# Pooled attention into a snake MLP on one core: k loaded by halves of the heads and ahead of the moves, q paired to suit, and the rest of the first batch moved

## Chip, core, metric

The kernel runs on one core of a Trainium2 chip. The metric is device microseconds of one execution. Engine names are those of the profile: PE is TensorE's matmuls, PEld its weight loads, DVE VectorE, ACT ScalarE, POOL GpSimd, and SPq the queue from which SyncE issues transfers.

## The reference

Attention pools k and v by means of 8 tokens (576 tokens to 72), and its output, reshaped to 4608 x 512, feeds an MLP with the activation h + sin(alpha h)^2 / alpha.

```python
def _attn_ref(q, k, v):                    # 8 batches, 8 heads, 576 tokens, 64 per head
    k_p = k.reshape(B, H, 72, 8, D).mean(axis=3)
    v_p = v.reshape(B, H, 72, 8, D).mean(axis=3)
    attn = softmax(q @ k_p^T / sqrt(D))    # abridged
    return attn @ v_p

def _moe_ref(x, w_in, w_out, alpha):       # 4608 x 512, 512 x 2048, 2048 x 512
    h = x @ w_in
    g = h + sin(alpha * h) ** 2 / (alpha + 1e-09)
    return g @ w_out
```

## The kernel before

The first MLP product runs in nine units, each of 28 slots of eight matmuls (1.73 us a slot at full clock). Attention of batch u + 1 is threaded through unit u: a table says at which slot each of its steps is put into the instruction streams. Every queue executes in the order of that table. "Cut" marks what is left out.

```python
def load_k(self, b, e):                    # half the heads of a batch: 4 heads x 24 rows of 6 KB
    t = self.kvp.tile([P, 2048], F32, name="kvin")[:NP * m, 0:3 * POOL * D]
    self.nc.sync.dma_start(out=t, in_=self.k[b].rearrange("(hp e) (p x) d -> e hp p (x d)", e=2, x=3 * POOL)[e])
    # cut: self.kp[b]
    self.pool_rows(t.rearrange("p (j x) -> p j x", j=3), self.kp[b][:, :, e, :])   # three additions on GpSimd

def move(part):                            # the softmax, transposed in blocks by VectorE, into place: 16 small transfers a batch
    for a in (2 * part, 2 * part + 1):
        for s in range(2):
            for c in range(2):
                nc.sync.dma_start(out=flat(self.aM[r:r + 32, a]), in_=flat(tr[32 * a:32 * a + 32, c, s]))

# the table for unit u, batch b = u + 1 (cut)
at((1, 3, 4, 5, 6)[i], A.score, i)         # scores and the subtraction of the maximum
at((8, 9, 10, 10, 10)[i], A.exp, i)
at((9, 10, 10, 10, 11)[i], A.norm, i)
at((11, 12, 12, 13, 13)[i], A.turn, i)     # VectorE's block transposes
at(13, A.move, 0)
at(13, A.move, 1)
at((0, 1)[i], self.load_v, b, i)
at((14, 15)[i], self.load_k, b + 1, i)     # behind the moves in the SP queue
at(25, lambda: A.values((0, 2, 1, 3), A.free_banks()))
at(26, self.att[b + 1].k_t)                # TensorE transposes the pooled k of the next batch
turn = 21                                  # q of batch u + 2: transposes on VectorE at slots 21, 22, transfers at 23, 24

# unit 0 also (cut)
at(2, A0.score, 4); at(2, A0.exp, 4); at(2, A0.norm_rest)    # the last 64 tokens of batch 0, its "rest"
at(3, self.root)                           # 1/sqrt(alpha): VectorE, a square root on ScalarE, VectorE
at((4, 10, 14)[J - 1], self.combine_w_in, J, 0)
at((6, 12, 15)[J - 1], self.combine_w_in, J, 1)              # three additions on VectorE, both inputs in SBUF
at((4, 5)[i], self.load_v, 1, i)
at(4, A.k_t)
at((17, 18)[e], self.load_k, 2, e)
```

Words used below: the *moves* are the 16 small transfers a batch that bring the softmax, transposed in blocks by VectorE, into place; *k_t* is TensorE's transpose of the pooled k; the *turn of q* is VectorE's transposes of q; *g* is what the activation gives, and its stores go out by the SP queue; the *rest* of batch 0 is its last 64 tokens. Matmuls are called cold where they take about twice their usual time, and warm otherwise. A line of a timeline gives start, duration, engine, line, operation, output and inputs, shapes and count; the bracket is the engine's idle time before it and what ended that.

Of the kernel before, what the change touches and what calls it, by code (L numbers as in the profile page):

```python
# [40 lines left out]
class Kernel:  # L41
# [40 lines left out]

    def load_q_pairs(self, b):

        self.new_q(b)
        x = self.q_pairs(self.qm[b])
        for t in range(4):
            self.nc.sync.dma_start(out=x[:, t], in_=self.q[b, :, 0:4 * P, :].rearrange("h (p t) d -> t p h d", t=4)[t])
        self.load_q_rest(b, x[:64, 4])

    def q_pairs(self, qm):
        return qm[:].rearrange("p (t h d) -> p t h d", t=5, h=self.H)

# [8 lines left out]
    def load_k(self, b, e):  # L102

        Sp, D, NP = self.Sp, self.D, self.NP
        m = Sp // 3
        t = self.kvp.tile([P, 2048], F32, name="kvin")[:NP * m, 0:3 * POOL * D]
        self.nc.sync.dma_start(out=t, in_=self.k[b].rearrange("(hp e) (p x) d -> e hp p (x d)", e=2, x=3 * POOL)[e])  # L107
        if b not in self.kp:
            self.kp[b] = self.ap.tile([NP * m, 3, 2, D], F32, name="kp")
        self.pool_rows(t.rearrange("p (j x) -> p j x", j=3), self.kp[b][:, :, e, :])  # L110
# [65 lines left out]
    def turn_q(self, b, part):  # L176
# [8 lines left out]
        if part < 2:  # L185
            for e in range(2):
                if part == 0:
                    out = tr[:, 2 * e:2 * e + 2, :, 0:4, :].rearrange("p k hp t i -> p hp t k i")
                    x = main[:, e::2].rearrange("p hp t (k i) -> p hp t k i", i=32)
                else:  # L190
                    out = tr[:64, 2 * e:2 * e + 2, :, 4, :].rearrange("p k hp i -> p hp k i")
                    x = rest[:, e::2].rearrange("p hp (k i) -> p hp k i", i=32)
                nc.vector.transpose(out=out, in_=x)
            return
# [17 lines left out]
    def attention(self, b):  # L212
# [4 lines left out]
        scale = 1.0 / (D ** 0.5) / POOL  # L217
        E = lambda n, i, h0, h1: ex[:n, i, h0:h1, 0:Sp]
        aT = []
# [9 lines left out]
        def q_t(i):  # L229

            n = rows[i]
            x = self.q_pairs(self.qm[b])[:n, i]
            if b not in self.qt:
                self.qt[b] = self.qt_view(self.qp.tile([P, 5 * H * D], F32, name="q"))
            ps = self.abank([P, NP, P])
            for hp in range(NP):
                nc.tensor.transpose(ps[:, hp, :n], x[:, 2 * hp:2 * hp + 2].rearrange("p h d -> p (h d)"), self.ident[:n, :n])
            nc.scalar.copy(out=self.qt_tiles(b)[:, i, :, :n], in_=ps[:, :, :n])
# [20 lines left out]
        def shift(i, e, ps):  # L259

            n = rows[i]
            mx = self.sm.tile([P, NP], F32, name="mx")
            nc.vector.tensor_reduce(out=mx[:n], in_=ps[:n], axis=AX, op=OP.max)
            nc.vector.tensor_tensor(out=ex[:n, i, e::2, 0:Sp], in0=ps[:n],
                                    in1=mx[:n].unsqueeze(2).to_broadcast([n, NP, Sp]), op=OP.subtract)
# [87 lines left out]
        def norm_rest():  # L353

            n = 64
            sm = self.sm.tile([P, H], F32, name="sm")
            nc.vector.tensor_reduce(out=sm[:n], in_=ex[:n, 4, :, 0:Sp + 1], axis=AX, op=OP.add)
            nc.vector.reciprocal(out=sm[:n], in_=sm[:n])
            for g in range(2):
                h = slice(4 * g, 4 * g + 4)  # L360
                m = sm[:n, h].rearrange("p (s e) -> p s e", s=2).unsqueeze(3).to_broadcast([n, 2, 2, 64])
                nc.vector.tensor_tensor(out=self.a4[:, 2 * g:2 * g + 2].rearrange("p e s k -> p s e k"),
                                        in0=ex[:n, 4, h, 0:64].rearrange("p (s e) k -> p s e k", s=2), in1=m, op=OP.mult)
            x = ex[:n, 4, :, 64:Sp].rearrange("p (hp e) k -> p hp e k", e=2)
            m = sm[:n].rearrange("p (hp e) -> p hp e", e=2).unsqueeze(3)
# [22 lines left out]
        def a_rest():  # L388

            aM, aR = a0_views()  # L390
            ps = self.abank([P, 5, 64])
            for j in range(4):
                nc.tensor.transpose(ps[:, j, :], self.a4[:, j].rearrange("p s k -> p (s k)"), self.ident[:64, :64])
            nc.tensor.transpose(ps[:, 4, :], self.z4.rearrange("p hp x k -> p (hp x k)"), self.ident[:64, :64])
            nc.scalar.copy(out=aM[:, :, 4 * P:], in_=ps[:, 0:4, :])
            nc.scalar.copy(out=aR[:, 4 * P:], in_=ps[:, 4, :])

# [36 lines left out]
        def value_parts(hp, rest):  # L434
# [3 lines left out]
            if b == 0:  # L438
                aM, aR = a0_views()
                w = slice(4 * P, S) if rest else slice(0, 4 * P)  # L440
                r = 32 * hp
# [314 lines left out]
    def first_batch(self):  # L756
# [19 lines left out]
        self.k2 = h[1][:self.Sp, n:n + m].rearrange("p (h u d) -> p h u d", h=self.H, u=2)  # L776
        self.a4 = h[1][:64, n:n + 512].rearrange("p (j s k) -> p j s k", j=4, s=2)
        self.z4 = h[1][:64, n + m:n + m + 128].rearrange("p (hp x k) -> p hp x k", hp=4, x=4)
        nc.gpsimd.memset(self.z4, 0.0)
# [9 lines left out]
        warm(4, 3)  # L789
        A.q_head(0)  # L790
        A.k_head(0)
        for hp in range(4):
# [8 lines left out]
            if hp:  # L801
                A.norm_head(hp - 1, nc.vector if hp == 1 else nc.gpsimd)
        self.load_q_rest(0, self.q_rest)
        for e in range(2):
            self.load_k(1, e)
        self.load_q_pairs(1)
        self.load_w_in_part(1)
# [10 lines left out]
    def carry(self, u):  # L818
# [5 lines left out]
        if u == 0:  # L824
# [6 lines left out]
            at(2, A0.score, 4)  # L831
            at(2, A0.exp, 4)
            at(2, A0.norm_rest)
            at(2, self.load_w_in_part, 2)
            at(3, self.root)
            at(4, A0.a_rest)
            at(6, lambda: A0.values_rest((5, 6, 7, (self.turn + 1) % 5)))
            for J in range(1, 4):
# [3 lines left out]
            for i in range(2):  # L842
                at((4, 5)[i], self.load_v, 1, i)
            at(4, A.k_t)
            for i in range(5):
# [12 lines left out]
            for e in range(2):  # L858
                at((17, 18)[e], self.load_k, 2, e)
            at(26, self.att[2].k_t)  # L860
            turn = 22
        else:
            at(0, self.sums_of_x, u, 2)
            at(0, self.sums_of_x, u, 3)
        if 0 < u < last:
# [9 lines left out]
            for i in range(2):  # L875
                at((0, 1)[i], self.load_v, b, i)
                if b < last:
                    at((14, 15)[i], self.load_k, b + 1, i)
            at(25, lambda: A.values((0, 2, 1, 3), A.free_banks()))
# [3 lines left out]
            if u + 3 <= last:  # L883
                at(7, self.load_q, u + 3)
            turn = 21
        elif u:
# [212 lines left out]
    def run(self):  # L1099
        nc, tc = self.nc, self.tc  # L1100
        pool = lambda s, n, b, **kw: s.enter_context(tc.tile_pool(name=n, bufs=b, **kw))
        with ExitStack() as top:
# [8 lines left out]
            with ExitStack() as one:  # L1111
# [13 lines left out]
                for i in range(2):  # L1125
                    self.kblk.append(cb.tile([P, self.NP, self.Sp], F32, name=f"kblk{i}"))
                self.ex = cb.tile([P, 5, self.H, 80], F32, name="ex")
                nc.gpsimd.memset(self.ex[:, :, :, self.Sp:], 0.0)
                nc.gpsimd.memset(self.ex[:, :, :, self.Sp:self.Sp + 1], 1e-9)
                self.twos = cb.tile([P, 64], F32, name="twos")  # L1130
                self.eights = cb.tile([64, 32], F32, name="eights")
                self.mask = cb.tile([P, 4], F32, name="mask")
                nc.vector.tensor_reduce(out=self.twos[:], in_=ident[:].rearrange("p (m k) -> p m k", k=2), axis=AX, op=OP.add)
                x = ident[:64, :64].rearrange("p (m k) -> p m k", k=8)
# [71 lines left out]
```

## Time and profile before

| what | before |
|---|---|
| median of the first three runs | 1005.29 us |
| span of the profiled run | 1007.4 us |
| first batch, until slot 0 of unit 0 | 28.2 us |
| unit 0, from slot 0 to the k_t at its end | 85.3 us, 12.7 of it waiting |
| units 1 to 5, from k_t to k_t | 68.3 us each |
| from the last k_t to the end | 552.6 us |

The times of these stages are starts of instructions in the timeline of TensorE. The page's first two parts show the engines' busy time with its share of the span, and the granted clock in tenths over 40 slices of 25 us:

```profile
PE 932.8 (93%) x6949; PEld 831.7 (83%) x6949; DVE 688.2 (68%) x1068; ACT 437.1 (43%) x1005; POOL 144.5 (14%) x146
...
PEclk9999799899998998998999999999999999999999
```

TensorE looks almost full, but the clock falls below 0.9 in five slices of the first half. In each of them stands the k_t of a unit, which waits, and the prediction shows one.

### The profile page before, as it was taken

The numbers are of one execution on the slowest core, as the hardware profiler recorded it, in microseconds if no ns is written. First come the engines' busy times: TensorE is split into PE (matmuls) and PEld (weight loads), VectorE is DVE, ScalarE is ACT, GpSimd is POOL, SyncE is SP. The second block draws the span as 40 slices with busy tenths as digits, with TensorE's granted clock in tenths as the row PEclk, the third lists the DMA queues.
The fourth block names the chain that finished last, engine by engine and source line by source line (L and its number), as shares of the span: only waits on it lengthen the run. The fifth ranks groups of instructions, "written<-read, shape, count | busy, mean of one in ns | idle before, by whom it ended". The sixth has DMA issues, their size and how long they took to land.

```text
span 1007.4 us, 17655 instructions
## 1 busy us (share of the span) xinstructions
PE 932.8 (93%) x6949; PEld 831.7 (83%) x6949; DVE 688.2 (68%) x1068; ACT 437.1 (43%) x1005; POOL 144.5 (14%) x146
## 2 busy tenths in 40 slices
PE   8889499797997997989999999999999999999997
PEld 7677477675875775767778889999999999999997
DVE  6785374563663754736635588998888797979795
ACT  3556276374574663754768765111111111111111
POOL 4340241232222403423200000000000000000000
PEclk9999799899998998998999999999999999999999
DMA  8846445645635646155373263535261716262511
GB/s 211 202 132 200 129 139 146 185 119 161 188 102 180 180 127 185 68 157 169 88 256 130 88 224 131 150 87 188 49 210 29 209 37 200 51 197 67 169 25 36
DMA packets 144251, 141.12 MB, mean 140 GB/s; under 512 B 53784, under 2 KB 113960, under 8 KB 144168
## 3 DMA queue, kind: packets, MB, share of 16 engines
q1 hardware_dynamic: 143096, 138.81, 46.6%
q10 hardware_dynamic: 1072, 1.19, 0.4%
q8 instruction: 55, 0.90, 0.4%
q14 instruction: 28, 0.23, 0.1%
HBM read 75.37 MB, written 47.19 MB: 122 GB/s over the span
## 4 chain that ended last, share of the span: by engine, by line
PE 70%; DMA 10%; DVE 7%; SPq 6%; ACT 2%; POOL 2%; issue 2%; DVEq 0%; ACTq 0%; POOLq 0%
PE PS L964 38%; PE PS L671 27%; DMA kvin<-in_k_dram 9%; SPq L416 5%; PE PS L256 2%; POOL kvin L116 2%; DVE tr L404 1%; DVE h L650 1%; DMA g_bridge<-h 1%; DVE sm L285 1%; DVE h L738 1%; ACT s L684 1%; DVE tr L405 1%; PE PS L767 1%; SPq L107 0%
## 5 line engine op out<-in xcount | busy, mean ns | idle before, releaser
L671 PE MATMUL PS<-home,a 128*128 128x256 f32 x1152 | 271.9, 387 | 12.9 <-DVE h L650 12.9
L671 PEld LDWEIGHTS PS<-home,a 128*128 128x128 f32 x1152 | 219.8, 194 | 53.3 <-DVE h L650 15.7
L671 PE MATMUL PS<-home,as 128*128 128x256 f32 x864 | 211.4, 396 | 1.3 <-ACT PS L697 0.9
L671 PEld LDWEIGHTS PS<-home,as 128*128 128x128 f32 x864 | 168.8, 198 | 26.7 <-ACT PS L697 1.3
L650 DVE TENSOR_TENSOR h<-PS,p 128x512 f32<-128x512 f32 x72 | 49.4, 685 | 131.5 <-DMA g_bridge<-h 55.8
L677 ACT ACTIVATE s<-h,al 128x256 f32<-128x256 f32 x144 | 65.3, 501 | 126.0 <-DVE h L650 126.0
L964 PE MATMUL PS<-s,wb 128*128 128x144 f32 x896 | 119.3, 286 | 0.4 <-ACT PS L1077 0.4
L964 PEld LDWEIGHTS PS<-s,wb 128*128 128x128 f32 x896 | 113.7, 190 | 0.7 <-ACT PS L1077 0.6
L684 ACT ACTIVATE s<-s,c 128x256 f32<-128x256 f32 (+1 forms) x216 | 110.0, 572 | 0.0
L116 POOL TENSOR_TENSOR kvin<-kvin 96x768 f32<-96x768 f32 (+3 forms) x42 | 66.0, 1572 | 265.8 <-DMA kvin<-in_k_dram 161.6
L1077 ACT COPY PS<-PS 128x144 f32<-128x144 f32 x56 | 14.7, 263 | 145.7 <-PE PS L964 144.3
L964 PE MATMUL PS<-s,a 128*128 128x144 f32 x512 | 73.2, 286 | 0.0
L964 PE MATMUL PS<-r,wb 128*128 128x144 f32 x512 | 73.2, 286 | 0.0
L677 ACT ACTIVATE s<-PS,al 128x256 f32<-128x256 f32 x144 | 60.2, 469 | 28.6 <-PE PS L671 11.2
L964 PEld LDWEIGHTS PS<-r,wb 128*128 128x128 f32 x512 | 67.1, 190 | 0.1
L964 PEld LDWEIGHTS PS<-s,a 128*128 128x128 f32 x512 | 67.0, 190 | 0.0
L738 DVE TENSOR_TENSOR h<-PS,s 128x512 f32<-128x512 f32 x36 | 24.6, 683 | 54.8 <-ACT s L684 54.7
L964 PE MATMUL PS<-s,we 128*128 128x144 f32 x384 | 54.9, 286 | 0.0
L964 PE MATMUL PS<-x,wb 128*128 128x144 f32 x384 | 54.9, 286 | 0.0
L1096 ACT COPY PS<-PS 128x144 f32<-128x144 f32 x56 | 14.7, 263 | 88.5 <-PE PS L964 88.5
L964 PEld LDWEIGHTS PS<-s,we 128*128 128x128 f32 x384 | 50.3, 190 | 0.1
L964 PEld LDWEIGHTS PS<-x,wb 128*128 128x128 f32 x384 | 50.3, 190 | 0.0
(162 smaller groups left out, 1202.4 us busy)
## 6 DMA issues: line engine op xcount, KB each, us to landing
g_bridge<-h SPq DMA_DIRECT2D x72, 512.0 KB
r<-g_bridge SPq DMA_DIRECT2D x31, 1152.0 KB
out_dram<-o SPq DMA_DIRECT2D x128, 72.0 KB
kvin<-in_k_dram SPq DMA_DIRECT2D x14, 576.0 KB
kvin<-in_v_dram SPq DMA_DIRECT2D x14, 512.0 KB
q<-in_q_dram SPq DMA_DIRECT2D x6, 1024.0 KB
aM<-tr SPq DMA_DIRECT2D x56, 100.0 KB
aM<-tr SPq DMA_DIRECT2D x56, 80.0 KB
```

Of the source, the lines that this page charges most:

```text
L116: self.nc.gpsimd.tensor_tensor(out=t[..., 0:w] if w > D else out, in0=t[..., 0:w], in1=t[..., w:2 * w], op=OP.add)
L256: nc.tensor.matmul(ps[e][r:r + q.shape[-1], hp, :], q[s], k, start=True, stop=True)
L285: nc.vector.tensor_reduce(out=sm[:n], in_=ex[:n, i, :, 0:Sp + 1], axis=AX, op=OP.add)
L416: nc.sync.dma_start(out=flat(self.aM[r:r + 32, a]), in_=flat(tr[32 * a:32 * a + 32, c, s]))
L650: add = lambda o, x, y: nc.vector.tensor_tensor(out=o, in0=x, in1=y, op=OP.add)
L671: nc.tensor.matmul(ps[:, jj, :], self.A[p][:, kk, f * P:(f + 1) * P], x[:, kk, :], start=(start and jj == 0 and kk == 0), stop=(kk == 1), ...
L677: nc.scalar.activation(out=G.s[:, i, jj, j, :], in_=src[:, jj], func=AF.Sin, scale=self.al[:, f:f + 1])
L684: nc.scalar.activation(out=x, in_=x, func=AF.Square, scale=self.c[:, f:f + 1])
L738: add = lambda o, x, y: self.nc.vector.tensor_tensor(out=o, in0=x, in1=y, op=OP.add)
L964: nc.tensor.matmul(out, W[:, J // 2, J % 2, :], A[:, J, :], start=(start and J == 0), stop=(J == self.NJ - 1), skip_group_check=True)
L1077: nc.scalar.copy(out=x1[:, 0, :], in_=x0[:, 1, :])
L1096: nc.scalar.copy(out=x1[:, 1, :], in_=x1[:, 0, :])
```

## The change

Its intent is in four parts. k comes earlier: its two loads go ahead of the moves. k comes by halves of the heads (0 to 3, then 4 to 7) instead of alternate heads, so q must be paired (h, h + 4). The load of q of batch 1, made of 256-byte pieces, becomes a plain one (but for its last 64 tokens), with five pairing copies on ScalarE. The rest of batch 0 gets a tile of its own and is spread over unit 0.

```diff
 # load_k
-        ... in_=self.k[b].rearrange("(hp e) (p x) d -> e hp p (x d)", e=2, x=3 * POOL)[e])
+        ... in_=self.k[b, NP * e:NP * e + NP].rearrange("h (p x) d -> (h p) (x d)", x=3 * POOL))
 # turn_q and shift, for batches 1 to 7
-                    x = main[:, e::2].rearrange("p hp t (k i) -> p hp t k i", i=32)
+                    x = main[:, 4 * e:4 * e + 4].rearrange("p hp t (k i) -> p hp t k i", i=32)
 # q of batch 1: load_q_pairs goes, and on ScalarE comes
+    def pairs_q(self, b, tiles):   # cut: self.raw is q as loaded, x the paired tile
+            nc.scalar.copy(out=x[:n, t], in_=raw.rearrange("p (e h) d -> p e h d", e=2))
 # first batch
         A.q_head(0)
+        warm(2, 4)
         A.k_head(0)
         self.load_q_rest(0, self.q_rest)
+        self.load_q(1)
         for e in range(2):
             self.load_k(1, e)
-        self.load_q_pairs(1)
 # unit 0
-            at(2, A0.exp, 4)
-            at(2, A0.norm_rest)
-            at(4, A0.a_rest)
-            at(6, lambda: A0.values_rest((5, 6, 7, (self.turn + 1) % 5)))
+            at(9, A0.exp, 4)
+            at(12, A0.norm_rest)
+            at(15, A0.a_rest)
+            at(18, lambda: A0.values_rest((5, 6, 7, (self.turn + 1) % 5)))
+            at(2, self.pairs_q, 1, (0, 1))
+            at(3, self.pairs_q, 1, (2, 3, 4))
-                at((4, 5)[i], self.load_v, 1, i)
-            at(4, A.k_t)
+                at((6, 7)[i], self.load_v, 1, i)
+            at(5, A.k_t)
-                at((17, 18)[e], self.load_k, 2, e)
+                at((12, 12)[e], self.load_k, 2, e)
-            turn = 22
+            turn = 23
 # units 1 to 6
-                    at((14, 15)[i], self.load_k, b + 1, i)
+                    at(11, self.load_k, b + 1, i)
-            turn = 21
+            turn = 22
```

Cut here: the spare tiles themselves, and the views that go with them.

More of the change, by code (lines that the diff above doesn't have):

```diff
@@ L81, in load_q_heads @@
                                in_=self.q[b, h0:h1, 0:4 * P, :].rearrange("h (p t) d -> p h (t d)", t=4))
-    def load_q_pairs(self, b):
-        self.new_q(b)
-        x = self.q_pairs(self.qm[b])
-        for t in range(4):
-            self.nc.sync.dma_start(out=x[:, t], in_=self.q[b, :, 0:4 * P, :].rearrange("h (p t) d -> t p h d", t=4)[t])
-        self.load_q_rest(b, x[:64, 4])
-    def q_pairs(self, qm):
-        return qm[:].rearrange("p (t h d) -> p t h d", t=5, h=self.H)
+    def pairs_q(self, b, tiles):
+        nc = self.nc
+        if 0 in tiles:
+            self.raw = self.q_views(self.qm[b])
+            self.qm[b] = self.qp.tile([P, 5 * self.H * self.D], F32, name="q")
+        x = self.qm[b][:].rearrange("p (t h e d) -> p t e h d", t=5, e=2, d=self.D)
+        for t in tiles:
+            n = P if t < 4 else 64
+            raw = self.raw[0][:, :, t, :] if t < 4 else self.raw[1]
+            nc.scalar.copy(out=x[:n, t], in_=raw.rearrange("p (e h) d -> p e h d", e=2))
     def load_q_rest(self, b, at=None):
@@ L106, in load_k @@
         t = self.kvp.tile([P, 2048], F32, name="kvin")[:NP * m, 0:3 * POOL * D]
-        self.nc.sync.dma_start(out=t, in_=self.k[b].rearrange("(hp e) (p x) d -> e hp p (x d)", e=2, x=3 * POOL)[e])
+        self.nc.sync.dma_start(out=t, in_=self.k[b, NP * e:NP * e + NP].rearrange("h (p x) d -> (h p) (x d)", x=3 * POOL))
         if b not in self.kp:
@@ L188, in turn_q @@
                     out = tr[:, 2 * e:2 * e + 2, :, 0:4, :].rearrange("p k hp t i -> p hp t k i")
-                    x = main[:, e::2].rearrange("p hp t (k i) -> p hp t k i", i=32)
+                    x = main[:, 4 * e:4 * e + 4].rearrange("p hp t (k i) -> p hp t k i", i=32)
                 else:
                     out = tr[:64, 2 * e:2 * e + 2, :, 4, :].rearrange("p k hp i -> p hp k i")
-                    x = rest[:, e::2].rearrange("p hp (k i) -> p hp k i", i=32)
+                    x = rest[:, 4 * e:4 * e + 4].rearrange("p hp (k i) -> p hp k i", i=32)
                 nc.vector.transpose(out=out, in_=x)
@@ L217, in attention @@
         scale = 1.0 / (D ** 0.5) / POOL
-        E = lambda n, i, h0, h1: ex[:n, i, h0:h1, 0:Sp]
+        row = lambda i: 5 if b == 0 else i
+        E = lambda n, i, h0, h1: ex[:n, row(i), h0:h1, 0:Sp]
         aT = []
@@ L231, in q_t @@
             n = rows[i]
-            x = self.q_pairs(self.qm[b])[:n, i]
+            x = self.qm[b][:n].rearrange("p (t hp x) -> p t hp x", t=5, hp=NP)[:, i]
             if b not in self.qt:
@@ L236, in q_t @@
             for hp in range(NP):
-                nc.tensor.transpose(ps[:, hp, :n], x[:, 2 * hp:2 * hp + 2].rearrange("p h d -> p (h d)"), self.ident[:n, :n])
+                nc.tensor.transpose(ps[:, hp, :n], x[:, hp], self.ident[:n, :n])
             nc.scalar.copy(out=self.qt_tiles(b)[:, i, :, :n], in_=ps[:, :, :n])
@@ L263, in shift @@
             nc.vector.tensor_reduce(out=mx[:n], in_=ps[:n], axis=AX, op=OP.max)
-            nc.vector.tensor_tensor(out=ex[:n, i, e::2, 0:Sp], in0=ps[:n],
+            nc.vector.tensor_tensor(out=ex[:n, row(i), e::2, 0:Sp] if b == 0 else ex[:n, i, 4 * e:4 * e + 4, 0:Sp], in0=ps[:n],
                                     in1=mx[:n].unsqueeze(2).to_broadcast([n, NP, Sp]), op=OP.subtract)
@@ L356, in norm_rest @@
             sm = self.sm.tile([P, H], F32, name="sm")
-            nc.vector.tensor_reduce(out=sm[:n], in_=ex[:n, 4, :, 0:Sp + 1], axis=AX, op=OP.add)
+            nc.vector.tensor_reduce(out=sm[:n], in_=ex[:n, 5, :, 0:Sp + 1], axis=AX, op=OP.add)
             nc.vector.reciprocal(out=sm[:n], in_=sm[:n])
@@ L362, in norm_rest @@
                 nc.vector.tensor_tensor(out=self.a4[:, 2 * g:2 * g + 2].rearrange("p e s k -> p s e k"),
-                                        in0=ex[:n, 4, h, 0:64].rearrange("p (s e) k -> p s e k", s=2), in1=m, op=OP.mult)
-            x = ex[:n, 4, :, 64:Sp].rearrange("p (hp e) k -> p hp e k", e=2)
+                                        in0=ex[:n, 5, h, 0:64].rearrange("p (s e) k -> p s e k", s=2), in1=m, op=OP.mult)
+            x = ex[:n, 5, :, 64:Sp].rearrange("p (hp e) k -> p hp e k", e=2)
             m = sm[:n].rearrange("p (hp e) -> p hp e", e=2).unsqueeze(3)
@@ L388, in a_rest @@
         def a_rest():
-            aM, aR = a0_views()
             ps = self.abank([P, 5, 64])
@@ L394, in a_rest @@
             nc.tensor.transpose(ps[:, 4, :], self.z4.rearrange("p hp x k -> p (hp x k)"), self.ident[:64, :64])
-            nc.scalar.copy(out=aM[:, :, 4 * P:], in_=ps[:, 0:4, :])
-            nc.scalar.copy(out=aR[:, 4 * P:], in_=ps[:, 4, :])
+            nc.scalar.copy(out=self.last_t[:], in_=ps)
         def turn(i):
@@ L438, in value_parts @@
             if b == 0:
-                aM, aR = a0_views()
-                w = slice(4 * P, S) if rest else slice(0, 4 * P)
+                aM, aR = (self.last_t[:, 0:4], self.last_t[:, 4]) if rest else a0_views()
+                w = slice(0, 64) if rest else slice(0, 4 * P)
                 r = 32 * hp
@@ L776, in first_batch @@
         self.k2 = h[1][:self.Sp, n:n + m].rearrange("p (h u d) -> p h u d", h=self.H, u=2)
-        self.a4 = h[1][:64, n:n + 512].rearrange("p (j s k) -> p j s k", j=4, s=2)
-        self.z4 = h[1][:64, n + m:n + m + 128].rearrange("p (hp x k) -> p hp x k", hp=4, x=4)
+        self.a4 = self.last[:64, 0:512].rearrange("p (j s k) -> p j s k", j=4, s=2)
+        self.z4 = self.last[:64, 512:640].rearrange("p (hp x k) -> p hp x k", hp=4, x=4)
         nc.gpsimd.memset(self.z4, 0.0)
@@ L1126, in run @@
                     self.kblk.append(cb.tile([P, self.NP, self.Sp], F32, name=f"kblk{i}"))
-                self.ex = cb.tile([P, 5, self.H, 80], F32, name="ex")
+                self.ex = cb.tile([P, 6, self.H, 80], F32, name="ex")
                 nc.gpsimd.memset(self.ex[:, :, :, self.Sp:], 0.0)
@@ L1132, in run @@
                 self.mask = cb.tile([P, 4], F32, name="mask")
+                self.last = cb.tile([64, 640], F32, name="last")
+                self.last_t = cb.tile([P, 5, 64], F32, name="last_t")
                 nc.vector.tensor_reduce(out=self.twos[:], in_=ident[:].rearrange("p (m k) -> p m k", k=2), axis=AX, op=OP.add)
```

## The prediction

> **What bounds the kernel now.** I read the page first: TensorE (PE) is busy 93% of the span, so at most some 75 of 1007.4 us are its idle time. The chain that ended last says what the rest hangs on:
>
> ```profile
> PE 70%; DMA 10%; DVE 7%; SPq 6%; ACT 2%; POOL 2%; issue 2%; DVEq 0%; ACTq 0%; POOLq 0%
> PE PS L964 38%; PE PS L671 27%; DMA kvin<-in_k_dram 9%; SPq L416 5%; PE PS L256 2%; POOL kvin L116 2%; DVE tr L404 1%; DVE h L650 1%; DMA g_bridge<-h 1%; DVE sm L285 1%; DVE h L738 1%; ACT s L684 1%; DVE tr L405 1%; PE PS L767 1%; SPq L107 0%
> ```
>
> Beside the matmuls stands the load of k (9%), the SP queue issuing the moves of line 416 (5%) and the pooling of k on GpSimd (2%). The waits, of TensorE and of GpSimd, say how often and how long:
>
> ```profile
> POOL kvin L116 <- DMA kvin<-in_k_dram: 161.6, 14, 27.3
> ...
> PE PS L226 <- POOL kp L116: 45.8, 6, 12.7
> ```
>
> Line 226 is the transpose of the pooled k for the next batch (k_t). Six times, once per unit 0 to 5, TensorE sits idle there, 45.8 us in all: 12.7 in unit 0 and 6.2 to 7.1 in the others. One unit in order of time, from the SP queue, then from TensorE:
>
> ```profile
> 346.52 0.88 SPq L745 DMA_DIRECT2D g_bridge<-h  x2
> 357.61 10.89 SPq L416 DMA_DIRECT2D aM<-tr  x16
> 368.60 1.51 SPq L107 DMA_DIRECT2D kvin<-in_k_dram  x2
> 370.21 0.96 SPq L745 DMA_DIRECT2D g_bridge<-h  x2
> 372.87 13.74 SPq L200 DMA_DIRECT2D q<-tr  x8
> ```
>
> The queue does nothing from 347.40 to 357.61: its next instruction is the first move, which waits for VectorE's transposes. Then 16 moves take 10.89 us to issue. Only then, at 368.60, can the load of k go out, and now it shares the engines with a store of g and the q moves of line 200, and lands at 377.9 and 383.6.
>
> ```profile
> 379.07 0.46 PE L478 MATMUL PS<-aM,vm 64*64 64x64 f32 x16
> 379.47 0.66 PE L481 MATMUL PS<-aM,vz 32*128 32x64 f32 x8
> 387.21 0.74 PE L226 MATMUL PS<-ident,kp 96*128 96x96 f32 x3 [7.09 <-POOL kp L116]
> 387.75 3.67 PE L671 MATMUL PS<-home,as 128*128 128x256 f32 x8
> 391.22 3.70 PE L671 MATMUL PS<-home,a 128*128 128x256 f32 x16
> ```
>
> The reader should see two costs: 7.09 us idle, and then 8 matmuls in 3.67 us where 8 normally take 1.9. The table of windows has the clock at 0.50 in 386 to 390 us and 0.83 in 390 to 394.
>
> There is a control inside the same trace. The last unit with attention (after 454.84) loads no k. From its k_t to the end of its last values (516.56) are 61.7 us, with one idle piece only (1.83 us, behind VectorE line 650), though its moves also go out late (494.1 to 505.1).
>
> **What the Trainium skill says.** "TensorE: Matmul & The Clock Gate", Part 1: the array drops to half clock after about 3.4 us of idleness and needs about as long of work to come back. The trace agrees: the 1.83 us pause leaves the next matmuls at their usual pace, the 7.09 us one is followed by the doubled times above. "DMA: Bandwidth & Descriptors", Why small descriptors are slow: pieces of 256 bytes from HBM carry a fixed overhead. The old load of q of batch 1 is made of such pieces; its five issues hold the SP queue from 19.4 to 35.1 us, against 1.0 us (0.37 + 0.65) for a plain load of q at 56.28. "SBUF — State Buffer", Who interferes with whom: a VectorE instruction with two SBUF inputs and a GpSimd one that reads SBUF exclude each other. The trace agrees: line 644 takes 0.69 us normally and 2.29 and 1.48 us at 33.9 and 36.2, while GpSimd pools k. "ScalarE: Activation LUTs", What ACT_TABLE_LOAD costs: about 1.28 us; every table load here shows 1.28.
>
> **The change, part by part.**
>
> 1. k ahead of the moves (slot 11 instead of 14/15; slot 12 instead of 17/18 in unit 0). Its two issues fall in the hole of the SP queue from 347.4 on. In the same stretch the DMA engines have one store of g (1.05 MB) until about 350.4 at roughly 380 GB/s and then nothing until the moves. k is 2 x 576 KB = 1.18 MB; an estimate at between that rate and the 157 GB/s that k and the store of g got together after 369.4 makes 3 to 8 us, so it lands by 351 to 358. GpSimd finishes its softmax products at 353.9, then pools twice 3.5 us, ready by 365 at the latest; TensorE asks for it at 380. The slack is 15 us, so the wait goes to zero in all six units: **-45.8 us**.
>
> 2. Without the idleness the clock stays up. The 24 matmuls after each k_t take 7.29, 7.36, 7.20, 7.19, 6.96 and 7.28 us in the chain, 43.3 in all; warm, 16 take 3.45 from start to start, so 24 take 5.2 and six times that 31.1: **-12.2 us**. k_t itself shows 0.74 us cold and 0.47 warm (at 42.31), six times 0.27: **-1.6 us**.
>
> 3. q turned one slot later (22 instead of 21). VectorE now stands 3.19 us in front of line 193 until the moves have read the tile; a slot is 1.73 us, so most of that goes. It is beside other work: 0. The 16 q moves then start at about 375 and, issued at 0.65 us each without k in the way, end near 386; the scores need their last quarter at slot 5 of the next unit, in the new time about 393. No new wait.
>
> 4. Halves of the heads instead of alternate heads; (h, h+4) in the pairing. The same rows of 6 KB, the same count and shape of instructions: 0.
>
> 5. Plain load of q for batch 1, paired by ScalarE. Five copies of up to 128x512, by line 711's 0.59 us: +2.9 us on ScalarE in slots 2 and 3, where it is idle 5.81 us (before 39.36) waiting for VectorE. Frees about 14 us of the SP queue; k of batch 1 goes out near 20.5 instead of 14.2, pooled by about 39 against 38.1, and k_t is asked for at about 42: 0.
>
> 6. Rest of batch 0 spread out. In the old order TensorE waits 2.41 us (39.22 to 41.63) for the products of line 362, plus 0.43 us at 43.20, and is then cold: 8 matmuls from 44.10 take about 3.1 instead of 1.73 us (1.4), 4 transposes 0.9 instead of 0.45. That is -4.7. Against it norm_rest (0.75 + 0.20 + 2 x 0.68 + 0.21, about 2.5 us of VectorE) moves to slot 12, where VectorE is full: 5.0 of 5 us busy in 70 to 75 and 4.93 in 75 to 80, and TensorE already waits 1.96 us there for line 650 and goes cold. I put all of it on the path: +2.5. Two more warming matmuls at the start: +0.3. Sum about **-2 us**.
>
> Total: 45.8 + 12.2 + 1.6 + 2 = 61.6. I give back 3 us, because GpSimd's pooling of k (7 us) now falls beside a busy VectorE, whose line 650 has under 1 us of slack before TensorE feels it (half a us per unit, an estimate). About -58.6: 1005.3 - 58.6 = 946.7. A check by periods: the k_t of unit 0 starts at 113.48 and of unit 5 at 454.84, so 68.3 us per unit; the control unit without its cold start is 61.7 - 2.4 = 59.3. Five periods save 45, the control's own cold start 2.4, unit 0 12.7 + 2: 62 again.
>
> **Rivals.** (a) The wait moves to the next late transfer. VectorE's line 650 waits 55.8 us in six times for stores of g, up to 11.5, in the same hole. If that were independent of k, TensorE would stall there and little would be won (about 990). Against it: the store in question is issued at 370.21 behind moves and k and lands at 386, while stores with free engines take 3.7 to 3.9 us in the chain. It is late because of k and the q moves. (b) The moves come late, because k takes their bandwidth, so that values at slot 25 (374.2) wait. Their readers are released at 370.15, 4 us earlier, and by then k has landed. A full collision would cost some 4 us in each of six units: 970. (c) A busier array could be throttled. Against it: from 516 to 626 us PE is busy 109.7 of 110 us, ScalarE 77, VectorE 70, with the clock at 1.00. If it happened anyway at 0.95, the 400 us up to slot 25 of the last unit would give back 20 us: 966. (d) Unit 0's VectorE jam grows by more than the 2.5 us: 949 to 952.
>
> **Range and chances.** The mechanism (a late load with an idle engine behind it, with a control that lacks it) is plain, and even half of it is over 2%. The range goes from everything won and unit 0 better than thought (938) to one of the rivals b or c in part (963).
>
> **What would show it.** Right: no wait of line 226 for kp of more than a few tenths; the issue of k directly after the store of slot 10 and before the 16 moves; period of a unit about 59.5 to 60.5 us; clock 1.00 right after k_t; PE idle total down from 75 to under 30 us; phases after the attention unchanged (about 491 us from there to the end). Step 6 wrong: the gap in front of line 650 at slots 13 to 15 of unit 0 much over 4.5 us. Prediction wrong: TensorE waiting at slot 25 for aM, at slots 1 to 5 for q, or at line 671 for line 650 some us in each unit.

## The result, and the profile after

The changed kernel takes 956.10 us in the median (954.52 to 958.38, four runs) against 1004.82 for the kernel before beside it. Its ratio is 0.9509, with a 95% interval of 0.9472 to 0.9546. Every ratio here is from the fast runs of both kernels in the same rounds, so it is not quite the ratio of the medians quoted. The prediction of 946.7 us (938 to 963) holds: faster, inside its range, but 48.7 us won by the medians where 58.6 were expected.

The page of the changed kernel, the same two parts and then the chain that ended last by engine and line:

```profile
PE 917.7 (96%) x6953; PEld 819.3 (86%) x6953; DVE 695.5 (73%) x1068; ACT 439.1 (46%) x1009; POOL 151.2 (16%) x146
...
PEclk9989999999999999999999999999999999999999
...
PE 83%; DVE 3%; DMA 2%; ACT 1%; issue 1%; SPq 0%; DVEq 0%; ACTq 0%
```

The chain now holds 2% DMA instead of 10, and the issues of the SP queue are gone from it. The clock stays up after the first slices, with one digit left at 8. TensorE's idle time is 953.7 - 917.7 = 36 us, from 74.6. Its busy time fell by 15 us too, because fewer matmuls ran at half clock.

One unit of the changed kernel, from the SP queue (start, duration, line, count):

```profile
310.83 0.87 SPq L745 DMA_DIRECT2D g_bridge<-h  x2
311.80 2.03 SPq L108 DMA_DIRECT2D kvin<-in_k_dram  x2
321.92 11.15 SPq L416 DMA_DIRECT2D aM<-tr  x16
333.17 6.63 SPq L745 DMA_DIRECT2D g_bridge<-h  x4
```

The loads of k stand where the queue used to do nothing, 10 us before the first move. On TensorE, at the end of the same unit:

```profile
343.78 0.66 PE L481 MATMUL PS<-aM,vz 32*128 32x64 f32 x8
344.37 0.47 PE L228 MATMUL PS<-ident,kp 96*128 96x96 f32 x3
344.67 1.92 PE L671 MATMUL PS<-home,as 128*128 128x256 f32 x8
```

The k_t follows the values at once, and the eight matmuls behind it take 1.92 us instead of 3.67. Where the 53.7 us between the two profiled spans came from, stage by stage:

| stage | before | after | won | prediction |
|---|---|---|---|---|
| first batch, to slot 0 | 28.20 | 24.43 | 3.8 | -0.3 |
| unit 0, slot 0 to k_t | 85.28 | 82.27 | 3.0 | about 15 (wait 12.7, step 6), less 0.5 given back |
| units 1 to 5 | 341.4 | 297.0 | 44.4 | about 44.6, less 2.5 given back |
| last k_t to the end | 552.6 | 550.0 | 2.5 | 2.3 |

So everything expected of the regular units came, and unit 0 fell short by more than 11 us. (The cold matmuls behind the k_t of unit 0 stand in the row of units 1 to 5.) Unit 0 lost its wait of 12.66 us and still hardly became shorter. Three lines of TensorE in it, after the change (the bracket is the idle time before, and what ended it):

```profile
48.08 1.89 PE L671 MATMUL PS<-home,a 128*128 128x256 f32 x8
53.77 0.50 PE L258 MATMUL PS<-kblk,q 64*64 64x72 f32 x2 [3.80 <-DVE ex L266]
...
56.40 3.78 PE L671 MATMUL PS<-home,a 128*128 128x256 f32 x8
```

TensorE waits 3.80 us for VectorE and is then cold: 3.78 us for eight matmuls. On VectorE just before, in the changed kernel:

```profile
48.23 1.75 DVE L537 TENSOR_TENSOR as<-as,a 128x512 f32<-128x512 f32 x1
49.91 1.75 DVE L537 TENSOR_TENSOR a<-a,a 128x512 f32<-128x512 f32 x1
51.58 1.21 DVE L537 TENSOR_TENSOR as<-a,as 128x512 f32<-128x512 f32 x1
```

The same three additions in the kernel before:

```profile
51.48 0.68 DVE L537 TENSOR_TENSOR as<-as,a 128x512 f32<-128x512 f32 x1
52.07 0.69 DVE L537 TENSOR_TENSOR a<-a,a 128x512 f32<-128x512 f32 x1
52.68 0.68 DVE L537 TENSOR_TENSOR as<-a,as 128x512 f32<-128x512 f32 x1
```

They took 4.71 us instead of 2.05, and the scores' subtractions stand behind them. GpSimd tells what lay beside them, in the changed kernel:

```profile
47.07 4.04 POOL L117 TENSOR_TENSOR kvin<-kvin 128x1024 f32<-128x1024 f32 x2 [9.23 <-DMA kvin<-in_v_dram]
```

It is the pooling of v of batch 1. In the kernel before it began as the last of the additions ran out (at 53.36):

```profile
53.00 3.93 POOL L116 TENSOR_TENSOR kvin<-kvin 128x1024 f32<-128x1024 f32 x2 [14.93 <-DMA kvin<-in_v_dram]
```

The SP queue, through with k and q sooner, sends v at 35.62 instead of 40.08, and v lands early enough to collide. The two issues, first before, then after:

```profile
40.08 1.29 SPq L127 DMA_DIRECT2D kvin<-in_v_dram  x2
35.62 1.28 SPq L128 DMA_DIRECT2D kvin<-in_v_dram  x2
```

### The profile page after: what moved, and what is told of

It is laid out like the page before. It is cut to its first block, busy times and chain, and to the rows that moved or that the text cites. A ratio compares the mean times of both kernels' runs of the same rounds, so it can differ in the third digit from the quotient of the medians.

```text
span 953.7 us, 17665 instructions
## 1 busy us (share of the span) xinstructions
PE 917.7 (96%) x6953; PEld 819.3 (86%) x6953; DVE 695.5 (73%) x1068; ACT 439.1 (46%) x1009; POOL 151.2 (16%) x146
## 4 chain that ended last, share of the span: by engine, by line
PE 83%; DVE 3%; DMA 2%; ACT 1%; issue 1%; SPq 0%; DVEq 0%; ACTq 0%
PE PS L967 40%; PE PS L671 38%; PE PS L258 2%; DMA g_bridge<-h 2%; PE PS L456 1%; DVE h L738 1%; PE PS L458 1%; ACT s L684 1%; DVE sm L287 1%; PE PS L481 0%; DVE h L650 0%; PE PS L478 0%; ACT PS L697 0%; PE PS L228 0%; SPq L745 0%
## 5 line engine op out<-in xcount | busy, mean ns | idle before, releaser
L671 PEld LDWEIGHTS PS<-home,a 128*128 128x128 f32 x1152 | 217.4, 192 | 52.1 <-DVE h L650 15.7
L671 PE MATMUL PS<-home,as 128*128 128x256 f32 x864 | 202.2, 383 | 1.7 <-ACT PS L697 0.9
L671 PEld LDWEIGHTS PS<-home,as 128*128 128x128 f32 x864 | 163.1, 191 | 24.9 <-ACT PS L697 1.3
L738 DVE TENSOR_TENSOR h<-PS,s 128x512 f32<-128x512 f32 x36 | 24.7, 685 | 59.6 <-ACT s L684 59.5
```

Source lines behind the costliest of these rows:

```text
L671: nc.tensor.matmul(ps[:, jj, :], self.A[p][:, kk, f * P:(f + 1) * P], x[:, kk, :], start=(start and jj == 0 and kk == 0), stop=(kk == 1), ...
L738: add = lambda o, x, y: self.nc.vector.tensor_tensor(out=o, in0=x, in1=y, op=OP.add)
```

## The experiments

Theory 1: the place of k in the SP queue is what pays, in all regular units. Its rivals are the layout of the load and the later turn of q. Theory 2: the added warming matmuls bring the clock up sooner in the first batch. Theory 3: in unit 0 the collision of VectorE and GpSimd takes back most of what was won. Theory 4: ScalarE's queue, with the pairing copies and the square root, does the other part. "Unit 0" is from its slot 0 to its k_t, "unit" the mean from k_t to k_t after it, both from the profile.

| run | median us | ratio to before | unit 0 | unit |
|---|---|---|---|---|
| before | 1005 to 1006 | 1 | 85.3 | 68.3 |
| changed | 956.10 | 0.9509 | 82.3 | 59.4 |
| a_order: before, k early only | 953.98 | 0.9479 | 71.7 | 61.0 |
| p_half: before, halves only | 969.04 | 0.9629 | 84.0 | 61.8 |
| p_turn: before, later turn only | 1006.32 | 1.0025 | 84.7 | 68.0 |
| b_klate: changed, k late | 969.15 | 0.9629 | 86.4 | 61.3 |
| l_turn21: changed, turn as before | 956.58 | 0.9507 | 84.1 | 59.4 |
| d_nowarm: changed, no added warming | 956.00 | 0.9499 | 84.5 | 59.4 |
| c_comb8: changed, additions at slot 8 | 949.67 | 0.9433 | 75.7 | 59.4 |
| h_both: c_comb8, root and pairing earlier | 950.80 | 0.9449 | 76.4 | 59.4 |
| i_split: c_comb8, root in two places, pairing earlier | 948.49 | 0.9432 | 74.6 | 59.4 |
| k_rest: c_comb8, rest of batch 0 early | 950.45 | 0.9458 | 76.6 | 59.4 |
| p_best: before, halves, k early, later turn | 951.19 | 0.9453 | 77.4 | 59.4 |
| j_old0: p_best, additions at slot 8 | 947.59 | 0.9421 | 72.9 | 59.4 |

### a_order

```diff
 # the kernel before
-                at((17, 18)[e], self.load_k, 2, e)
+                at((12, 12)[e], self.load_k, 2, e)
-                    at((14, 15)[i], self.load_k, b + 1, i)
+                    at(11, self.load_k, b + 1, i)
```

> The kernel before with one thing changed: the loads of k go to slots 12 (unit 0) and 11 (units 1 to 5), ahead of the moves. Old layout of k and q, old load of q of batch 1, turn of q at slot 21, rest of batch 0 early. Theory 1 (the place of k in the SP queue is what paid, in all six units): no wait of k_t over 0.5 us, a unit of 59.5 us and unit 0 shorter by its whole 12.7 us wait, so 945 to 950 us, a ratio near 0.943: faster than the whole change, whose other parts lose time in unit 0. Rival (the load of whole halves of the heads, or the later turn of q, is needed for k and q to land in time): k_t still waits 2 us or more per unit or the scores wait for q, over 965 us.

Measured: 953.98 us. The waits for k are gone, so two moved lines do the work of the whole change, and theory 1 holds so far. But the time is 4 us over the expectation, because a unit takes 61.0 us and not 59.5. A new wait stands at the end of each of them (the 16 moves took 13.74 us to issue instead of 11.15, VectorE stood 6.10 us in front of the turn of q, and with it the sums and the sines):

```profile
340.56 0.46 PE L478 MATMUL PS<-aM,vm 64*64 64x64 f32 x16 [0.98 <-ACT home L431]
```

### b_klate

```diff
 # the changed kernel: the two lines of a_order, undone
-                at((12, 12)[e], self.load_k, 2, e)
+                at((17, 18)[e], self.load_k, 2, e)
-                    at(11, self.load_k, b + 1, i)
+                    at((14, 15)[i], self.load_k, b + 1, i)
```

> The changed kernel with the loads of k back at slots 17/18 and 14/15, behind the moves; all else as changed. Theory 1: the waits of k_t return (6 to 7 us in units 1 to 5, 10 us or more in unit 0) with the cold matmuls behind them, some 1005 to 1012 us, no better than before. Rival (the contiguous halves land sooner by themselves): waits of 3 us or less, below 990 us.

Measured: 969.15 us, as the rival had it, but for unit 0. The waits of k_t are 0.6 to 1.5 us in units 1 to 5 and 7.13 in unit 0, 11.9 in all instead of 45.8. Some other part of the change also brings k sooner. That the place alone pays is refuted: it suffices, but is not needed for most of the gain.

### p_turn and p_half

```diff
 # p_turn, the kernel before
-            turn = 22
+            turn = 23
-            turn = 21
+            turn = 22
```

> With k late in the changed kernel, k_t waited 1.5 us in units 2 to 5 instead of 7, and the whole took 969 us: against both theories of that run. What is left: the later turn of q, or the layout. This is the kernel before with the turn of q one slot later and nothing else. Theory T (the q moves issued 4 us behind the loads of k held them up): the waits fall to 1 to 3 us, 970 to 980 us. Theory L (a load that runs over alternate heads keeps only a quarter of the DMA engines busy: the trace of before shows a DMA share of 0.25 and 100 to 104 GB/s from 380 to 384 us, that of the changed kernel with k late 0.95 to 1.06 and 359 to 409 GB/s): the waits stay at 6 us or more, 998 to 1006 us.

Measured: 1006.32 us, waits of 5.98 to 7.16 us in units 1 to 5 and 12.37 in unit 0. The turn does nothing that the runs show (interval of the ratio 0.9969 to 1.0080). One reading in the expectation is off: the 359 to 409 GB/s of the run with k late belong to 350 to 356 us, when the first half of k was already being pooled (from 349.40); with k in flight, from 346 to 349.4, the share was 0.93 to 0.99 at 259 to 270 GB/s. That still separates the theories.

```diff
 # p_half, the kernel before: load_k, turn_q and shift as in the change, and for q of batch 1
+        x = x.rearrange("p t (h e) d -> p t e h d", e=2)
         for t in range(4):
-            self.nc.sync.dma_start(out=x[:, t], in_=self.q[b, :, 0:4 * P, :]...[t])
+            for e in range(2):
+                self.nc.sync.dma_start(out=x[:, t, e], in_=self.q[b, 4 * e:4 * e + 4, 0:4 * P, :]...[t])
```

> The kernel before with the halves of the heads alone: k loaded by halves, q of batches 1 to 7 paired (h, h+4) to suit (the load of q of batch 1 takes ten issues instead of five), k still behind the moves, turn at slot 21, rest of batch 0 early. Theory L (16 engines instead of 4): both loads land within 9 us of their issue, waits of 1 to 3 us in units 1 to 5, 6 to 8 us in unit 0, 967 to 977 us. Theory T: waits as before, 1000 us or more.

Measured: 969.04 us, waits of 1.07 to 2.26 us and 7.19 in unit 0. The k_t that waited 7.09 us in the kernel before:

```profile
357.24 0.47 PE L229 MATMUL PS<-ident,kp 96*128 96x96 f32 x3 [2.02 <-POOL kp L119]
```

The layout did it. The clearest view of why is the table of windows at the same place of a unit, when the store of g has gone and k is in flight. First a_order, with k in the old layout (the columns are the window, the busy time of PE, PEld, DVE, ACT and POOL with instructions, then PEclk, DMA share, GB/s):

```profile
314.00:316.00 2.00, 2.00 (x11) 1.74 (x11) 2.00 (x6) 0.73 (x3) 0.34 (x1) 1.00 0.25 104
316.00:318.00 2.00, 2.00 (x11) 1.77 (x10) 2.00 (x5) 2.00 (x6) 0.00 (x0) 1.00 0.26 111
```

Then the changed kernel, with halves:

```profile
314.00:316.00 2.00, 1.78 (x9) 1.22 (x7) 1.79 (x6) 1.97 (x4) 2.00 (x3) 1.00 1.07 297
316.00:318.00 2.00, 0.40 (x2) 0.38 (x3) 1.97 (x5) 1.60 (x6) 1.51 (x2) 1.00 1.02 237
320.00:322.00 2.00, 2.00 (x11) 1.76 (x10) 1.90 (x5) 2.00 (x6) 1.84 (x3) 1.00 0.00 0
```

The old load keeps a quarter of the 16 DMA engines busy, at 104 to 111 GB/s. The new one keeps all of them busy, and by 320 it is done. The Trainium skill states the rule, in "DMA: Bandwidth & Descriptors", section Why a DMA increments its semaphore by 16 and not by 1: the number of engines is the largest up to 16 that divides the slowest dimensions of both access patterns. The old source is 4 heads x 24 rows beside a tile of 96 partitions, which gives 4; the new one is 96 rows in one dimension, which gives 16. The trace agrees with both numbers. This also explains a_order's longer units: its load, although early, is still running when the moves go out (issued at 307.92, its halves are pooled from 318.41 and 326.10, while the moves start at 318.04).

p_half also shows something that its expectation did not ask for. Unit 0 takes 84.0 us, hardly less than before, although its wait fell from 12.66 to 7.19 us. Its pooling of v and the three additions:

```profile
47.34 4.03 POOL L119 TENSOR_TENSOR kvin<-kvin 128x1024 f32<-128x1024 f32 x2 [13.39 <-DMA kvin<-in_v_dram]
48.29 1.96 DVE L540 TENSOR_TENSOR as<-as,a 128x512 f32<-128x512 f32 x1
50.17 1.75 DVE L540 TENSOR_TENSOR a<-a,a 128x512 f32<-128x512 f32 x1
51.85 1.21 DVE L540 TENSOR_TENSOR as<-a,as 128x512 f32<-128x512 f32 x1
```

So the collision of theory 3 is here too, without the plain load of q: v goes out at 34.28. In a_order and p_turn, which keep the old layout, v goes out at 38.89 and 39.98, and the additions take 0.68 or 0.69 us each.

### l_turn21

```diff
 # the changed kernel
-            turn = 23
+            turn = 22
-            turn = 22
+            turn = 21
```

> The changed kernel with the turn of q at slots 22 (unit 0) and 21 as before. Step 3 of the prediction gives the later turn nothing: 955.5 to 957 us and units of 59.4 us. Rival (with k early, VectorE standing in front of the moves holds back the sums of line 738 and through them ScalarE, as in the run with k early in the old layout, where line 478 waited 1 us or more per unit): units of 60.5 us or more, 961 us or more.

Measured: 956.58 us, units of 59.4. With halves the turn's slot is worth nothing, and with the turn where a_order has it the units are not longer; so the turn alone does not make a_order's.

### d_nowarm

```diff
         A.q_head(0)
-        warm(2, 4)
         A.k_head(0)
```

> The changed kernel without the two added warming matmuls. In the profile after the change, the transposes and products of the first 20 us ran at twice the speed of before. Theory 2 (the two matmuls fill a hole, so that the clock comes up at about 5 us instead of 20): without them the 32 products of line 329 take 1.24 us again instead of 0.73 and slot 3 of unit 0 starts 3 to 4 us later, 959 to 960 us. Rival (the clock came up early by chance, or the loads were sooner): no difference above 1 us, 956.

Measured: 956.00 us; the four runs of each kernel have the same mean, 956.27. Theory 2 falls: what the first batch "won" in the profile is chance. In this run the array was cold at the first of the four product groups (1.24 us for 32 products) and warm at the second (0.73). p_turn, which adds no warming, was warm at the first; h_both and k_rest, which have it, were cold until the fourth.

### c_comb8

```diff
 # the changed kernel
-                at((6, 12, 15)[J - 1], self.combine_w_in, J, 1)
+                at((8, 12, 15)[J - 1], self.combine_w_in, J, 1)
```

> The changed kernel with the second half of the first combination of w_in at slot 8 instead of 6 of unit 0, behind the pooling of v on GpSimd instead of beside it. Theory 3 (three VectorE additions with two SBUF inputs took 4.7 instead of 1.9 us beside GpSimd and delayed the scores by 3.8 us, and the clock fell): the wait of 3.8 us goes to under 1 us and the cold matmuls after it too, 950 to 952 us. Rival (the delay belongs to the ScalarE chain ahead of it, or shows up again at slot 8): 955 us or more.

Measured: 949.67 us, unit 0 shorter by 6.6 us. The place that waited 3.80 us now shows no bracket, and the eight matmuls behind are warm:

```profile
49.93 0.98 PE L258 MATMUL PS<-kblk,q 64*64 64x72 f32 x32
50.84 0.46 PE L239 MATMUL PS<-ident,q 64*128 64x64 f32 x4
51.23 2.00 PE L671 MATMUL PS<-home,a 128*128 128x256 f32 x8
```

Theory 3 holds. The pooling of v still begins at 47.21; the additions, now at 52.75, take 0.74, 0.80 and 1.09 us.

### h_both and i_split

What is left in c_comb8 at slot 5 is a stop of 1.26 us for VectorE's copy of k and 2.16 us for ScalarE's copy of q.

```diff
 # h_both: c_comb8, and
+            at(1, self.root)               # ahead of the sums of x
-            at(3, self.root)
-            at(2, self.pairs_q, 1, (0, 1))
-            at(3, self.pairs_q, 1, (2, 3, 4))
+            at(2, self.pairs_q, 1, (0, 1, 2, 3, 4))
```

> The changed kernel with three things moved in unit 0: the second half of the combination at slot 8 (which alone gave 949.7), the root of alpha at slot 1 ahead of the sums of x, all five pairing copies at slot 2. Theory 4 (the other stop at slot 5, 2.2 us for a copy of q on ScalarE and 1.3 for the copy of k on VectorE, comes from ScalarE standing behind root and three pairing copies): both waits under 0.5 us, the cold matmuls after them gone too, 943 to 947 us. Rival (they come from the PSUM banks or VectorE): 949 to 950 us, as without it.

Measured: 950.80 us, no gain over c_comb8. The wait for ScalarE's copy of q is gone and the one for VectorE's copy of k is 1.13 us, but ScalarE now stands 1.81 us in front of the square root at slot 1, and TensorE waits 2.44 us for the copy of line 317 behind it. This profile also has the late start of the clock.

```diff
 # i_split: as h_both, but root in two
+        self.root(0)                       # behind the copies of the first batch, up to the square root
+            at(3, self.root, 1)            # the rest
```

> The changed kernel with the combination at slot 8 (949.6 in the mean), all pairing copies at slot 2, and root cut in two: its first VectorE instructions and the square root behind the last copies of the first batch, the rest at slot 3. The run with the whole of root at slot 1 showed why that place was bad: ScalarE stood 1.8 us in front of the square root and the copy of line 317 behind it held TensorE for 2.4 us. Theory 4 (ScalarE's queue makes the stop at slot 5): the waits for the copy of q and of k there under 0.5 us in all, no new wait at slot 2, unit 0 shorter by 3 to 4 us, 945 to 947 us. Rival (what is won there is lost at the next stop, line 650 at slots 13 to 15): 948.5 to 950.

Measured: 948.49 us, at the lower edge of the rival's 948.5 to 950. Of the stop at slot 5 only 1.22 us is left, for the copy of k. Unit 0 is 1.1 us shorter than in c_comb8 and not 3 to 4, because TensorE arrives sooner at the next stop, VectorE's crowded slots 13 to 15:

```profile
64.98 3.72 PE L675 MATMUL PS<-home,a 128*128 128x256 f32 x16 [2.50 <-DVE h L654]
...
71.62 5.21 PE L675 MATMUL PS<-home,as 128*128 128x256 f32 x16 [2.47 <-DVE h L654]
```

So ScalarE did make the stop for q at slot 5. Repairing it is worth about 1 us by the medians, which is not clear of noise: the ratios are 0.9433 and 0.9432.

### k_rest

```diff
 # c_comb8, with the rest of batch 0 back
-            at(9, A0.exp, 4)          at(12, A0.norm_rest)    at(15, A0.a_rest)    at(18, ... A0.values_rest ...)
+            at(2, A0.exp, 4)          at(2, A0.norm_rest)     at(4, A0.a_rest)     at(6, ... A0.values_rest ...)
```

> The changed kernel with the combination at slot 8 and the rest of batch 0 where it was before (slots 2, 2, 4, 6), the spare tile kept. By the prediction's step 6 the spreading wins 4.7 us early and loses 2.5 late, so undoing it costs about 2 us: 951 to 952 against 949.6. Rival (the early wait was hidden behind the stop of ScalarE at slot 5, and the late additions are paid in full): 947 to 949.

Measured: 950.45 us, unit 0 76.6 us against 75.7. It leans to the prediction's 2 us, but the interval of its ratio (0.9437 to 0.9478) lies within that of c_comb8 (0.9386 to 0.9479), so whether spreading the rest pays anything stays open. The two profiles show both of its terms: with the rest early, slots 0 to 9 take 37.7 us against 33.6, and what follows takes 38.9 against 42.1. The comparison is not clean: here TensorE waits 3.33 us for the pairing copies, which stand behind the rest's exponential on ScalarE and which the kernel before did not have.

### p_best and j_old0

```diff
 # p_best: the kernel before, with a_order, p_half and p_turn together
 # j_old0: p_best, and
-                at((6, 12, 15)[J - 1], self.combine_w_in, J, 1)
+                at((8, 12, 15)[J - 1], self.combine_w_in, J, 1)
```

> The kernel before with halves of the heads, k at slots 12 and 11 and the turn one slot later; first batch and unit 0 otherwise as before (no pairing on ScalarE, rest of batch 0 not spread, no warming matmuls added). In the run with k early in the old layout, k_t of unit 0 came at 97.3 us, 9.5 us sooner than in the changed kernel, but a unit took 1.0 to 1.7 us longer, with a wait of line 478 for ScalarE behind it. Theory U (the other parts of the change lose time in unit 0; the longer units come from the slow load of k holding up the moves): units of 59.4 us, 943 to 948 us, faster than the changed kernel by 1%. Rival (the long units come from something else in the old first batch): 951 us or more.

Measured: 951.19 us. The units are 59.4 us, so (with l_turn21, which clears the turn) the layout was what a_order lacked. But unit 0 took 77.4 us and not 72, and the time lies just inside the rival's range. Here too v came early (pooled from 48.20), and the three additions took 1.12, 1.75 and 1.21 us.

> The kernel before with halves of the heads, k early, the turn one slot later and the combination at slot 8: no pairing on ScalarE, no spread rest, no added warming matmuls. Without the slot 8 this gave 950.7 in the mean, with waits for VectorE's line 267 of 2.3 us and cold matmuls behind them. If the collision of VectorE and GpSimd made those: 946 to 948 us, so that the pairing on ScalarE and the spread rest are worth nothing. If they were due to the ten issues for q of batch 1: 950 to 951.

Measured: 947.59 us, ratio 0.9421 with an interval of 0.9406 to 0.9436, the lowest median of all (not clear of c_comb8 and i_split), and clear of the changed kernel's 0.9472 to 0.9546. Its unit 0 takes 72.9 us, what the unit of before takes without its wait (85.28 - 12.66 = 72.6). The pairing on ScalarE, the plain load of q, the spread rest and the added warming are not needed for the gain; the halves, the earlier slots of k and the one moved slot of the additions are enough (the later turn rides along).

## Why the prediction was right, and where not

**Steps 1 and 2 (k early, the clock) were right** in the regular units to the microsecond: units of 59.39 us against 59.3 from the control, with no wait of k_t over 0.5. k landed 7 us after its issue, inside the 3 to 8 estimated; but that was luck, or step 4: in a_order, with the layout that the estimate was made for, the halves landed some 10 and 18 us after it, and the 15 us of slack took that up. Slot 25 never waited for the moves, so rival b did not happen, nor did rivals a and c: VectorE's waits for g fell from 55.8 us to 0.2, and the clock was at 1.00 through all the units. The 3 us given back for GpSimd beside line 650 in the regular units were not lost; that wait stayed at 1.82 us, as in the control unit before. One sign failed: TensorE's idle total was to fall below 30 us and is 36, some 13 of them in unit 0.

Two readings in the prediction need a word. It says that the trace agrees with 3.4 us of idleness for the fall of the clock, and shows pauses of 1.83 and 7.09 us. The same trace has a pause between them that does not fit, and step 6 itself counts it as cold:

```profile
70.47 5.41 PE L671 MATMUL PS<-home,a 128*128 128x256 f32 x16 [1.96 <-DVE h L650]
```

Sixteen warm ones take 3.62 to 3.72 us; the granted clock was 0.51 from 72 to 74 us. And its figure for a table load is the load alone: the section named there adds a drain and puts a whole switch at 2.66 us. In the trace of before ScalarE went on 0.12 us after the load at 41.06 was over. Nothing in the sum rests on it.

**Step 4 (halves: "0") was wrong.** The working counts rows and bytes, which are the same, and not the engines that carry them. Alone it wins 36 us (p_half). It did not spoil the total because it and step 1 remove the same wait: with either, k_t waits little, and the sum is not their sum (before 1005, early 954, halves 969, both 951). The page named above has the rule, and the profile of before showed the symptom: between 380 and 384 us the DMA share was 0.25, with k the load being waited for. The prediction does not mention it.

**Step 3 (later turn: 0) was right in its sum**, shown twice. Its reason was not: VectorE's wait in front of the turn was to go for the most part, and stayed at 15.4 us in five times (3.55 us in the unit shown).

**Step 5 (plain load of q: "0") missed what cost most, and so did step 4.** The working of step 5 saw that the SP queue gains 14 us (q of batch 1 held it for 15.7 us before and 5.0 after) and that k and q would still be in time. It did not ask what else moves up: v. v came early and its pooling fell on three VectorE additions with two SBUF inputs. 6.6 us of unit 0 were that (c_comb8), although the prediction cites the very exclusion two paragraphs earlier, and charges it to the regular units, where it did nothing. The plain load is not needed for the collision: p_half and p_best, which have the halves and ten issues for q, show it too. By these runs it takes v going out some 4 us sooner, and either part does that; whether with halves it is the faster k or the ten issues, no run separates. The five copies on ScalarE were put into 5.81 us of idleness in front of the rest's exponential, which step 6 moved elsewhere; the stop for q's copy (2.08 us) came from them and the square root, worth about 1 us at most in the end (i_split).

**Step 6 (rest of batch 0: -2 us) did not show in unit 0.** Rival d did not happen: the late jam did not grow by more than 2.5 us. Slots 10 to the end, without the wait of k_t, lost 1.8 us, once the 1.6 us of matmuls that moved there are set aside (37.65 us became 41.1), and the waits for line 650 at slots 13 to 15 are 1.95 and 0.79 us. The early term, -4.7, was swallowed by the collision: slots 0 to 9 grew from 35.0 to 40.7 us, and shrank to 33.6 in c_comb8. What step 6 is worth stays open (k_rest). The added warming matmuls, put at +0.3, cost nothing that the runs show, and the 3.8 us of the first batch are chance.

So the total came inside the range for the reasons given in the regular units, and the more than 11 us missed in unit 0 were small enough to fit into it.

## What to carry to other kernels

When a transfer is late, ask both when it is issued and how many DMA engines it uses; a low DMA share while somebody waits for one load (here 0.25) can mean a load on few engines. After freeing a queue, list everything behind the freed place, not only the load in mind, and look what each item will run beside when it arrives sooner. Two repairs of one wait do not add up: test each alone before keeping both, and before keeping parts that only ride along.

## What the Trainium skill lacked or had wrong

- "TensorE: Matmul & The Clock Gate", Part 1, puts the warm-up at about 3.4 us of sustained work and its variation at the phase of a window. At the start of this kernel, with TensorE busy some 80 to 90% in pieces, the first warm group of products began anywhere from 7.0 to 20.8 us in fourteen profiles, with or without two more matmuls; up to 4 us of the span depend on it. The profile's granted clock said 1.00 throughout the first 20 us of before, while 32 products took 1.24 us instead of 0.73, so here it does not show this state at a start. As to the fall to half clock, which the page puts after an idle window of about 3.4 us: pauses of 1.96 us (before, 70.47), 2.44 (h_both, 37.39) and 2.47 (i_split, 71.62) were followed by cold matmuls, and pauses of 1.83 (before, 489.72), 2.18 (a_order, 65.81) and 2.50 (i_split, 64.98) were not; the length of the last pause alone did not decide it.
- "SBUF — State Buffer", Who interferes with whom, was right that VectorE additions with two SBUF inputs exclude GpSimd reads and others do not (1.75 us against 0.68 for line 537; 0.69 as ever for line 650, whose input is in PSUM), but gives no size for a stream of them, only factors from single measurements: here three took 4.71 us instead of 2.05.
